# GpSimd's last shift of a D tile as one addition in place of a multiplication by 1.0 and an addition

## The chip, the core and the metric

The kernel runs on one core of a Trainium2 chip. The metric is the device time of one execution, in microseconds. The engines are TensorE (PE, matrix products; PEld is its loading of weights), VectorE (DVE), ScalarE (ACT), GpSimd (POOL) and SyncE (SP, which issues the transfers). They run their own lists of instructions in order and wait for one another through semaphores.

## What is computed

A residual block: x plus attention of the normalized x plus a dense layer with GELU of the same normalized x. There are 2048 rows of width 512, 32 query heads of width 16 over one shared key and value head, and a hidden width of 1792.

```python
x = A_x
xn = _layernorm(x, axis=-1)
return x + _A_ref(xn, A_wq, A_wk, A_wv, A_wo) + _B_ref(xn, B_w1, B_b1, B_w2, B_b2)
# _A_ref
scores = jnp.einsum("bhqd,bkd->bhqk", q, k) * (Dh ** -0.5)
p = _softmax(scores, axis=-1)
o = jnp.einsum("bhqk,bkd->bhqd", p, v)
# _B_ref
h = _gelu(jnp.einsum("bsd,df->bsf", h_in, w1) + b1)
return jnp.einsum("bsf,fd->bsd", h, w2) + b2
```

## The kernel before

**Tiles.** The scores are cut into tiles of 128 keys by 512 queries of one head. Four heads make a group; a group has 4 x 16 = 64 tiles, and 4 blocks of 512 queries by 8 groups make 32 groups, so there are 2048 tiles. They are worked off three at a time (`scores(u)`, `exp(u)`): three products into three banks of PSUM, with the two halves of six banks in turn.

**Two ways to the exponential.** `DTAB` says for each tile which engine turns its scores into weights. Most tiles go to ScalarE, which computes the exponential into `E` (L981). The others, the D tiles, go to VectorE: `p1` (L1012) turns the scores into 16-bit integers whose bits, read as bfloat16, are a rough power of two. One such number is too rough, so a D tile is used in five versions, each the first one plus a constant, and each multiplied by its own copy of V, already scaled by a constant of `SPL_C`. The sum of the five products makes a good exponential. The constants are `SPL_K = (-26, 0, 26, 51, 77)`.

**The shifts.** Up to six D tiles are collected in `batch`. `close_batch` then goes through three steps, each (out, in, number of buffers, constant):

```python
SPL_STEPS = ((1, 0, 1, 26), (2, 0, 2, 51), (0, 0, 1, -26))
```

The first two steps are VectorE's (L1059): buffer 1 becomes buffer 0 plus 26, and then buffers 2 and 3 become buffers 0 and 1 plus 51. The third step works in place: buffer 0 loses 26. It goes tile by tile (128 partitions by 512 int16), and by the program's rule it is GpSimd's (L1055, the kind `pl`). It can start once L1059 and TensorE have read the old buffer 0; after it, one more PV product per tile reads the new buffer 0.

**PV products.** `pv_mm` (L1025) adds V times a tile to the open bank `pO`, for four heads side by side. A product is planned by `allow=4.0`, as due 4.0 us after its operand is there. Buffer 0 is a ring of `ND = 19` tiles, the others are rings of `NR = 11`.

**What sets the order.** All work is first recorded by `add`, then `schedule` runs it through a table of planned durations and writes down each engine's list; `emit` turns the planned dependences into semaphore waits. For the shift the plan has `PL_OCC = 0.62` us. The planner places a GpSimd shift under a long VectorE instruction that reads PSUM (0.4 us or more), and has it wait until the VectorE instruction ahead (`gate`) has ended, so that GpSimd and VectorE's fast instructions between SBUF tiles (marked `lock`) do not overlap much. Where no such place is found in time, the planner gives the shift to VectorE: the same line, recorded with the same function. Of 557 shifts, 459 are on GpSimd and 98 on VectorE.

**Other work of GpSimd.** Two multiplications for each pair of groups (L1102), which divide the attention output by its sums, and the setting up of constants and masks in the first 28 us. Among the latter are the five scaled copies of V (L914, a multiplication by a constant), a mask times a number per partition (L921), a product with a constant for the layer norm (L762), all three with no second operation, and one small multiplication and addition (L722).

**The rest.** TensorE fits the projections of Q (L1139 empties them), the dense layer and the output projection in between, in the bank `pM`. A few products with zeros (L1336) stand where TensorE would pause.

Of the kernel before, what the change touches and what calls it, by code (L numbers as in the profile page):

```python
# [7 lines left out]
ALU = mybir.AluOpType  # L8
# [94 lines left out]
def vcost(n, mode=1):  # L103
    return n / 0.96e3 / mode + 0.065
# [7 lines left out]
class Prog:  # L112
# [19 lines left out]
    def add(self, eng, fn, r=(), w=(), acc=None, dma=None, occ=0.1, lat=0.15, allow=1.0, kind=None, tag=None, after=(), due=None, lock=False, docc=0.0):  # L132
        op = _Op()
        op.lock, op.docc = lock, docc
        op.eng, op.fn = eng, fn
        op.stream = dma or eng
        op.amt = 16 if dma else 1
        op.need = bool(dma)
        op.ticket = None
        op.occ, op.lat, op.allow, op.kind, op.tag = occ, lat, allow, kind, tag  # L140
        op.idx = len(self.ops)
        op.done = False
        op.due = due
        op.rel = None
        op.pm = any(k == ("bank", 7) or k[0] == ("bank", 7) for k in w)
        deps, sdeps = {}, {}

        def dep(o, raw):
            if o is None or o is op:
                return  # L150
            if o.stream == eng == "pe":
                sdeps.setdefault(id(o), (o, False))
                return
            deps[id(o)] = o
            sdeps[id(o)] = (o, True)

        for k in r:
            dep(self.writer.get(k), True)
            for o in self.accs.get(k, ()):
                dep(o, True)  # L160
        for k in w:
            dep(self.writer.get(k), False)
            for o in self.readers.get(k, ()):
                dep(o, False)
            for o in self.accs.get(k, ()):
                dep(o, False)
        if acc is not None:
            dep(self.writer.get(acc), False)
            for o in self.readers.get(acc, ()):
                dep(o, False)  # L170
        op.deps = list(deps.values())
        for o in op.deps:
            o.need = True
        for k in w:
            self.writer[k] = op
            self.readers[k] = []
            self.accs[k] = []
        for k in r:
            self.readers.setdefault(k, []).append(op)
        if acc is not None:  # L180
            self.accs.setdefault(acc, []).append(op)
        for o in after:
            sdeps.setdefault(id(o), (o, True))
        if self.in_chain:
            o = self.chain.get(eng)
            if o is not None:
                sdeps.setdefault(id(o), (o, False))
            self.chain[eng] = op
        op.sdeps = list(sdeps.values())
        self.ops.append(op)  # L190
        return op
# [344 lines left out]
def bass_parallel_sum__grouped_kv_mqa__dense_activation_gelu__prompt_kernel(  # L536
# [33 lines left out]
    with ExitStack() as es:  # L570
# [76 lines left out]
        add = pr.add  # L647
# [6 lines left out]
        def dve(fn, r=(), w=(), n=TBW, mode=1, allow=1.0, **kw):  # L654
            return add("dve", fn, r, w, occ=vcost(n, mode), lat=dlat[0], allow=allow, **kw)
# [27 lines left out]
        for i in range(8):  # L683
            e = X_Q[i]
# [251 lines left out]
        def tile_of(t):  # L936
            gg, r = divmod(t, TPG)
            return gg, r // HG, r % HG
# [26 lines left out]
        def exp(u):  # L965
# [20 lines left out]
            while ds:  # L986
                if not batch:
                    size[0] = bsize[ds[0][0]]
                n = 1
                while n < len(ds) and len(batch) + n < size[0] and ds[n][1] == ds[0][1] + n:  # L990
                    n += 1
                op = p1(ds[:n], ts[0] // TPG)
                o = o or op
                del ds[:n]
                if len(batch) == size[0] and batch[0][0] // TPG == ts[0] // TPG:
                    close_batch()
# [27 lines left out]
        def pv_mm(gg, j, v, kt, rhs, r):  # L1024
            add("pe", lambda e, a, b: e.matmul(pO[32 * j:32 * j + 32, :], V1[:, v, kt, :], rhs, start=a, stop=b,  # L1025
                                               tile_position=(0, 32 * j)),
                r=r + [("V", v, 0 if kt < NVA else NVA)], acc="O", occ=0.216, lat=dlat[1],
                allow=4.0 if gg < NTB * NGR - 1 or kt < NT - 4 else -5.0, kind="pv", tag=(gg, j))

        def close_batch():  # L1030
            n = len(batch)
            have = {0: 0}

            def slot(b):
                return base[0] if b == 0 else ND + (b - 1) * NR + base[1]

            def view(b, nb):
                s = slot(b)
                step = (slot(b + 1) - s if nb > 1 else n) * TBW
                return bass.AP(Dt[:].tensor, Dt[:].offset + s * TBW, [list(Dt[:].ap[0]), [step, nb], [1, n * TBW]])  # L1040

            def sums(bufs):
                for b in bufs:
                    v = 1 + SPL_K.index(have[b])
                    for q, (t, _) in enumerate(batch):
                        gg, kt, j = tile_of(t)
                        pv_mm(gg, j, v, kt, Dt[:, slot(b) + q, :].bitcast(bf), [(("D", base[b > 0] + q), b)])

            for o, i, nb, k in SPL_STEPS:
                def keys(b):  # L1050
                    return [(("D", base[b + m > 0] + q), b + m) for m in range(nb) for q in range(n)]
                if o == i:
                    for q in range(n):
                        d = Dt[:, slot(o) + q, :]
                        add("pool", lambda e, d=d, k=k: e.tensor_scalar(d, d, 1.0, float(k), ALU.mult, ALU.add),  # L1055
                            [], [(("D", base[o > 0] + q), o)], occ=PL_OCC, lat=PL_LAT, allow=PL_DUE, kind="pl", lock=True,
                            docc=vcost(TBW, 4))
                else:
                    dve(lambda e, d=view(o, nb), q=view(i, nb), k=k: e.tensor_scalar(d, q, float(k), None, ALU.add),  # L1059
                        r=keys(i), w=keys(o), n=nb * n * TBW, mode=4, allow=1.0, kind="post", lock=True)  # L1060
                for m in range(nb):
                    have[o + m] = have[i + m] + k
                sums(range(o, o + nb))
            del batch[:]
# [220 lines left out]
        for u in range(NU):  # L1285
            ts = list(range(3 * u, min(3 * u + 3, NTILE)))
            exp(u)
            if u + 2 < NU:
                scores(u + 2)
            for t in ts:  # L1290
                gg, kt, j = tile_of(t)
                if not is_d[t]:
                    pv_mm(gg, j, 0, kt, E[:, eslot[t], :], [("E", eslot[t])])
                if t % TPG == TPG - 1:
                    assert all(b[0] > t for b in batch)
                    if gg == NTB * NGR - 1:
                        o_norm_last(gg)
                    else:
                        o_evac(gg)
            for a in nextg:  # L1300
                pv_mm(*a)
            del nextg[:]
            if batch and len(batch) == size[0]:
                close_batch()
            for gu, tbs in GU:
                if u == gu:
                    gelu(tbs, u)
            n0 = len(pr.ops)
            while side and side[0][0] <= u:
                side.pop(0)[2]()  # L1310
            for op in pr.ops[n0:]:
                op.sdeps.append((exps[u], True))
                op.rel = exps[u]
# [61 lines left out]
```

## Time and profile before

| | us |
|---|---|
| median of 3 runs (747.54 to 747.80) | 747.73 |
| the profiled execution, its own time | 747.55 |
| its span, first to last instruction | 745.8 |
| granted TensorE clock over the span | 1.00 |
| PE, DVE, ACT busy | 731.8, 732.7, 730.9 |
| POOL busy | 391.4 |
| DMA, mean | 31 GB/s |

How to read the profile: a group's line names the code line, the engine, the operation, what is written and read with its shape, how many there are, the busy time in us and the mean of one in ns, and after the second bar the idle time of the engine just ahead of them and what ended it. A line of the waits names who waited for whom, the sum in us, how often, and the longest. A line of the timeline has the start and the length in us, the instruction, how many were merged into the row, and in brackets the idle time ahead. Spans on GpSimd are rough; the spacing of instructions that follow each other is safer than the length of one.

### The profile page before, as it was taken

How to read it: one execution, taken by the hardware profiler on the slowest of the kernel's cores; microseconds unless marked ns; L12 is line 12 of the kernel's file. 1: busy time of each engine (PE TensorE's matmuls, PEld its weight loads, DVE VectorE, ACT ScalarE, POOL GpSimd, SP SyncE). 2: the span in 40 equal slices, each digit the busy share in tenths (PEclk: the TensorE clock that was granted, in tenths of full speed). 3: DMA queues.
4: the chain of work that ended last, by engine and by line, in shares of the span. 5: the costliest groups of instructions: out<-in, count | busy, mean ns of one | idle time of the engine just before them, and what ended most of it. 6: DMA issues, size and time to landing. Idle time of an engine off the chain costs nothing.

```text
span 745.8 us, 22104 instructions
## 1 busy us (share of the span) xinstructions
PE 731.8 (98%) x9048; PEld 218.3 (29%) x9050; DVE 732.7 (98%) x1432; ACT 730.9 (98%) x743; POOL 391.4 (52%) x543
## 2 busy tenths in 40 slices
PE   7999999999999999999999999999999999999998
PEld 5322222222232222222232222322333222222223
DVE  8899999999999999999999999999999999999997
ACT  8899999999999999999999999999999999999995
POOL 5455555656433556555555455465564545646541
PEclk9999999999999999999999999999999999999999
DMA  9200100100010010100101010100100101010011
GB/s 312 66 9 24 32 8 18 24 10 16 16 46 22 18 39 17 25 16 16 27 10 28 25 38 17 37 18 12 23 16 19 34 18 38 16 40 23 11 31 36
DMA packets 32078, 23.34 MB, mean 31 GB/s; under 512 B 16369, under 2 KB 27498, under 8 KB 31978
## 3 DMA queue, kind: packets, MB, share of 16 engines
q1 hardware_dynamic: 30922, 21.90, 11.2%
q8 instruction: 72, 1.18, 0.7%
q14 instruction: 28, 0.23, 0.1%
q10 hardware_dynamic: 1056, 0.03, 0.1%
HBM read 13.08 MB, written 2.35 MB: 21 GB/s over the span
## 4 chain that ended last, share of the span: by engine, by line
ACT 61%; PE 30%; DVE 7%; issue 0%; DMA 0%; SPq 0%; POOL 0%
ACT E L981 60%; PE pAll L1025 13%; PE pAll L958 9%; PE pAll L672 7%; DVE Dt L1012 3%; DVE Dt L1059 2%; DMA x_sb<-in_A_x_dram 0%; DVE x_sb L1167 0%; ACT x_sb L1179 0%; PE pAll L810 0%; DVE stats L759 0%; ACT xnT L815 0%; PE pAll L666 0%; DVE Dt L1055 0%; DVE Of L1071 0%
## 5 line engine op out<-in xcount | busy, mean ns | idle before, releaser
L981 ACT ACTIVATE E<-pAll 128x1024 bf16<-128x1024 f32 (+1 forms) x677 | 680.0, 1263 | 1.9 <-PE pAll L958 1.8
L1055 POOL TENSOR_SCALAR Dt<-Dt 128x512 int16<-128x512 int16 x459 | 350.7, 764 | 303.1 <-DVE Dt L1059 128.4
L1025 PE MATMUL pAll<-Dt,V 128*32 128x512 bf16 x2785 | 406.2, 383 | 0.9 <-DVE Of L1071 0.5
L1012 DVE TENSOR_SCALAR Dt<-pAll 128x512 int16<-128x512 f32 (+1 forms) x545 | 368.6, 691 | 2.1 <-PE pAll L958 1.0
L1025 PE MATMUL pAll<-E,V 128*32 128x512 bf16 x1491 | 293.1, 383 | 0.0
L1059 DVE TENSOR_SCALAR Dt<-Dt 128x1024 int16<-128x1024 int16 (+5 forms) x560 | 292.3, 548 | 0.2
L958 PE MATMUL pAll<-QT,KT 32*128 32x512 bf16 x2048 | 267.1, 384 | 4.1 <-ACT E L981 0.9
L958 PEld LDWEIGHTS pAll<-QT,KT 32*128 32x128 bf16 x2048 | 66.7, 91 | 293.9 <-ACT E L981 283.1
L1025 PEld LDWEIGHTS pAll<-Dt,V 128*32 128x32 bf16 x2785 | 102.0, 95 | 101.5 <-issue 68.2
L672 PE MATMUL pAll<-xnT,w_sb 128*32 128x512 bf16 x896 | 85.0, 383 | 0.1
L1025 PEld LDWEIGHTS pAll<-E,V 128*32 128x32 bf16 x1491 | 69.4, 94 | 44.3 <-issue 32.2
L672 PE MATMUL pAll<-w_sb,x_sb 128*32 128x512 bf16 x448 | 68.0, 383 | 0.0
L672 PE MATMUL pAll<-w_sb,ub 128*32 128x512 bf16 x448 | 67.1, 383 | 0.2 <-DVE x_sb L1213 0.2
L672 PE MATMUL pAll<-wop,oTp 128*32 128x512 bf16 x256 | 56.8, 383 | 0.0
L1102 POOL TENSOR_TENSOR oTp<-OfP,rbP 128x256 bf16<-128x256 f32 x29 | 24.1, 837 | 27.2 <-DVE Dt L1055 14.6
L672 PEld LDWEIGHTS pAll<-xnT,w_sb 128*32 128x32 bf16 x896 | 22.1, 95 | 27.0 <-issue 16.3
L1055 DVE TENSOR_SCALAR Dt<-Dt 128x512 int16<-128x512 int16 x98 | 25.7, 281 | 0.0
L672 PE MATMUL pAll<-xnT,wq_sb 128*32 128x512 bf16 x256 | 23.2, 384 | 0.2 <-DVE ub L1167 0.2
L1071 DVE COPY Of<-pAll 128x512 f32<-128x512 f32 x31 | 21.1, 679 | 0.0
L1167 DVE TENSOR_SCALAR x_sb<-pAll,b1T 128x512 bf16<-128x512 f32 x28 | 20.7, 741 | 0.0
L1167 DVE TENSOR_SCALAR ub<-pAll,b1T 128x512 bf16<-128x512 f32 x28 | 20.7, 738 | 0.1
L672 PEld LDWEIGHTS pAll<-w_sb,x_sb 128*32 128x32 bf16 x448 | 16.8, 95 | 10.3 <-issue 7.9
(121 smaller groups left out, 261.9 us busy)
## 6 DMA issues: line engine op xcount, KB each, us to landing
OfP<-Of SPq DMA_DIRECT2D x124, 32.0 KB, 2.0
rbP<-rden_rows SPq DMA_DIRECT2D x124, 32.0 KB, 1.8
w_sb<-in_B_w_dram SPq DMA_DIRECT2D x2, 1792.0 KB, 12.8
x_sb<-in_A_x_dram SPq DMA_DIRECT2D x8, 256.0 KB, 4.3
x_sb<-in_A_x_dram SPq DMA_DIRECT2D x16, 128.0 KB, 2.2
QT<-qp SPq DMA_DIRECT2D x124, 16.0 KB, 1.8
out_dram<-x_sb SPq DMA_DIRECT2D x12, 128.0 KB, 1.9
wq_sb<-in_A_wq_dram SPq DMA_DIRECT2D x1, 512.0 KB, 6.2
```

Source lines behind the costliest of these rows:

```text
L672: add("pe", lambda e, c=c, j=j: e.matmul(o[c, :], l[:, c], rh, start=start, stop=stop, tile_position=(0, 32 * j)), r, [(k, j) for k in w] ...
L958: ins = e.matmul(o, l, rh, start=True, stop=True, tile_position=(q0, 0))
L981: o = act(lambda e: e.activation(E[:, s0:s0 + na, :], bank(b0, na).rearrange("p (a n) -> p a n", a=na), ACT.Exp, scale=LN2 / 128.0), w=[B( ...
L1012: op = dve(lambda e: e.tensor_scalar(Dt[:, s:s + n, :], bank(bk, n).rearrange("p (a n) -> p a n", a=n), float(127 * 128) + SPL_D, SPL_MIN, ...
L1025: add("pe", lambda e, a, b: e.matmul(pO[32 * j:32 * j + 32, :], V1[:, v, kt, :], rhs, start=a, stop=b, tile_position=(0, 32 * j)), r=r + [ ...
L1055: add("pool", lambda e, d=d, k=k: e.tensor_scalar(d, d, 1.0, float(k), ALU.mult, ALU.add), [], [(("D", base[o > 0] + q), o)], occ=PL_OCC, ...
L1059: dve(lambda e, d=view(o, nb), q=view(i, nb), k=k: e.tensor_scalar(d, q, float(k), None, ALU.add), r=keys(i), w=keys(o), n=nb * n * TBW, m ...
L1071: dve(lambda e: e.tensor_copy(Of[:, i, :], pO), w=["O", ("Of", i)], allow=0.0)
L1102: "pool", lambda e, c=c: e.tensor_tensor(oTp[0:n, sl, c], OfP[0:n, s, c], rbP[0:n, s, c], ALU.mult),
L1167: dve(lambda e: e.tensor_scalar(ubs[tb % 2][:, ft, :], pM, b1T[:, ft:ft + 1], None, ALU.add), r=["b1T"], w=M4 + [ukey(tb, ft)], n=TBW + 57 ...
```

## The change

One line of `close_batch`. The in-place shift was `d = d * 1.0 + k`, two operations in one instruction; it is now `d = d + k`, one operation with the second absent. `k` is -26.0, the tile is 128 x 512 int16, read and written in place. The planned durations stay as they are, and the instructions of all engines stand in the same order as before, 459 of the shifts on GpSimd and 98 on VectorE.

```diff
                 if o == i:
                     for q in range(n):
                         d = Dt[:, slot(o) + q, :]
-                        add("pool", lambda e, d=d, k=k: e.tensor_scalar(d, d, 1.0, float(k), ALU.mult, ALU.add),
+                        add("pool", lambda e, d=d, k=k: e.tensor_scalar(d, d, float(k), None, ALU.add),
                             [], [(("D", base[o > 0] + q), o)], occ=PL_OCC, lat=PL_LAT, allow=PL_DUE, kind="pl", lock=True,
                             docc=vcost(TBW, 4))
                 else:
```

## The prediction

> **What bounds the kernel now.** I read the page first (its span, its busy shares, its chain of waits), then the groups by line and shape, then the waits, then single instructions in the timeline.
>
> ```profile
> span 745.8 us, 22104 instructions
> PE 731.8 (98%) x9048; PEld 218.3 (29%) x9050; DVE 732.7 (98%) x1432; ACT 730.9 (98%) x743; POOL 391.4 (52%) x543
> ACT 61%; PE 30%; DVE 7%; issue 0%; DMA 0%; SPq 0%; POOL 0%
> ...
> L1055 POOL TENSOR_SCALAR Dt<-Dt 128x512 int16<-128x512 int16 x459 | 350.7, 764 | 303.1 <-DVE Dt L1059 128.4 <-PE pAll L1025 61.3 <-DVE Dt L1012 39.8
> L1055 POOL TENSOR_SCALAR Dt<-Dt x459: 620/622/2059, 28.0 to 732.8; 128x512 int16<-128x512 int16 x153
> ...
> PEld pAll L958 <- ACT E L981: 283.1, 658, 0.9
> PEld pAll L1025 <- POOL Dt L1055: 2.7, 12, 0.2
> ```
>
> Three engines are 98% busy at once: TensorE, VectorE and ScalarE feed one another in a closed ring (scores, exponential or D tile, PV product, next scores). GpSimd is busy 52% of the span, and it has no share of the chain. The changed instruction is the whole of that work in the steady part: 459 shifts, the first at 28.0 us. A shift alone takes 622 ns (the median); the mean is 764. GpSimd stood idle for 303.1 us ahead of them, mostly because the tile or VectorE was not ready. TensorE waited for a shift 12 times, 2.7 us in all. So today a shift is covered, with 303 us of room in the sum; what matters is its price after the edit.
>
> **The change.** It moves nothing: the same instructions stand in the same order on every engine, since the planner's figure for a shift stays 0.62 us. In each shift the pair of operations becomes one, an addition with no second operation. Ninety-eight of the shifts run on VectorE, written by the same line:
>
> ```profile
> L1055 DVE TENSOR_SCALAR Dt<-Dt 128x512 int16<-128x512 int16 x98 | 25.7, 281 | 0.0
> L1059 DVE TENSOR_SCALAR Dt<-Dt 128x512 int16<-128x512 int16 x120 | 32.5, 283 | 0.1
> ```
>
> L1059 is already the form with one addition, and at this shape it takes 283 ns against 281. I cost those 98 at nothing.
>
> On GpSimd no 128x512 int16 shift with one operation is in the trace, so I go by what GpSimd did with both forms at the start of the kernel. L722 has two operations; L762, L914 and L921 have one (a multiplication, second operation absent). The copies are there to see what the shape and the type cost.
>
> ```profile
> L722 POOL TENSOR_SCALAR isc<-mrow 128x1 f32<-128x1 f32 x1 | 0.2, 192 | 0.0
> L762 POOL TENSOR_SCALAR nm<-sm 128x1 f32<-128x1 f32 x3 | 0.7, 217 | 2.2 <-ACT oTp L756 2.1
> L713 POOL COPY oTp<-wvk 128x256 bf16<-128x256 bf16 x1 | 0.4, 407 | 0.0
> L717 POOL CAST ident_f<-ident 128x128 f32<-128x128 bf16 x1 | 0.3, 299 | 0.0
> L921 POOL TENSOR_SCALAR sel8R<-sel,R 128x128 bf16<-128x128 bf16 x1 | 0.6, 600 | 0.0
> ...
> 24.00 0.85 POOL L914 TENSOR_SCALAR V<-oTp 128x256 bf16<-128x256 f32 x1
> ```
>
> Take off the fixed part, which the rows of one element show, and divide by the rest of the elements. With two operations: (622 - 192)/511 = 0.84 ns for each element. Copy: (407 - 192)/255 = 0.84; cast: (299 - 192)/127 = 0.84. With one operation: L914, (850 - 217)/255 = 2.48 ns; L921, (600 - 217)/127 = 3.02 ns. One operation costs three times as much for each element as two. The shape is not the reason, since the copy of L713 writes runs of 16 as L914 does, and neither is a change of type, since the cast runs at 0.84. What L914 and L921 share, and the fast rows lack, is the absent second operation. They multiply while the new shift adds, and neither has int16, so the step could fail there.
>
> I take L914, whose scalar is a constant as in the shift (L921 reads its scalar from a tile): 217 + 511 x 2.48 = 1484 ns. The upper bound is L921's rate, 217 + 511 x 3.02 = 1760 ns. The lower bound is a shift that stays at 622 ns or falls to some 217 ns, if one operation on int16 saves all the work for each element.
>
> The GPSIMD Engine Reference of the Trainium skill, section 3.1 (side-by-side cycle accounting), speaks against this: a body of up to two operations runs at the port's 1.03 cycles per element. By that rule both forms cost the same and the time stays where it is. The trace agrees for the two-operation shift and differs for L914, at 2.48 ns; that reading is a rival below.
>
> Next, what surrounds a shift. Two in a row, the five of L914 against VectorE's fourfold-rate shifts, and one case of such a shift starting inside a GpSimd shift:
>
> ```profile
> 34.48 1.32 POOL L1055 TENSOR_SCALAR Dt<-Dt 128x512 int16<-128x512 int16 x2 [5.25 <-DVE Dt L1059]
> ...
> 24.93 0.85 POOL L914 TENSOR_SCALAR V<-oTp 128x256 bf16<-128x256 f32 x1
> 25.86 0.90 POOL L914 TENSOR_SCALAR V<-oTp 128x256 bf16<-128x256 f32 x1
> 25.12 0.35 DVE L1059 TENSOR_SCALAR Dt<-Dt 128x512 int16<-128x512 int16 x1
> 25.50 0.55 DVE L1059 TENSOR_SCALAR Dt<-Dt 128x1024 int16<-128x1024 int16 x1
> ...
> 162.92 0.62 POOL L1055 TENSOR_SCALAR Dt<-Dt 128x512 int16<-128x512 int16 x1
> 163.12 0.69 DVE L1059 TENSOR_SCALAR Dt<-Dt 128x1024 int16<-128x1024 int16 x1
> L1059 DVE TENSOR_SCALAR Dt<-Dt 128x1024 int16<-128x1024 int16 x201 | 82.9, 419 | 0.1
> ```
>
> Two shifts take 1.32 us, so 0.08 us lies between them. The mean of 764 ns against 622 is another 0.14 us of stretch, from VectorE's L1059 and L1055: at 162.92 the shift held VectorE off until it ended (0.69 us against 0.42). Inside the slow L914 at 24.93 it was milder. The first L1059 took 0.35 us against 0.28 and ended in the middle of L914; the second took 0.55 against 0.42; and the next L914 took 0.90 against 0.85. I take half of the stretch, 0.07 us, and a spacing of 1.484 + 0.08 + 0.07 = 1.63 us. VectorE's own delay, 0.07 and 0.13 us here for two operations, I count at nothing, because where shifts are dense VectorE waits for TensorE anyway; uncovered it would be 658 x 0.1 = 66 us.
>
> Over the whole run GpSimd must then serve 459 x 1.63 = 748 us of shifts in the 717.8 us left after 28.0. It becomes the slowest engine, and the 303 us of room is used up. The shifts also come in bunches. TensorE runs its list in order, and the planner puts a shifted tile's PV product at most 4 us after the shift (the `allow=4.0` of `pv_mm`). So lateness up to about that is absorbed; beyond it TensorE stands at that product, the next scores are late, and ScalarE and VectorE starve. I therefore count by stretches of 4 us, over 40 us from the middle (columns of the page by stretches: window, length, VectorE's busy time in L1055, GpSimd's in L1055):
>
> ```profile
> 300.00:304.00 4.00, 0.00 (x0) 1.21 (x2) 1.00 0.00 0
> 304.00:308.00 4.00, 0.28 (x1) 2.93 (x3) 1.00 0.11 25
> 308.00:312.00 4.00, 0.28 (x1) 2.45 (x5) 1.00 0.16 29
> 312.00:316.00 4.00, 0.79 (x3) 2.30 (x4) 1.00 0.27 62
> 316.00:320.00 4.00, 0.35 (x2) 1.19 (x2) 1.00 0.00 0
> 320.00:324.00 4.00, 0.00 (x0) 0.00 (x0) 1.00 0.09 18
> 324.00:328.00 4.00, 0.00 (x0) 1.62 (x2) 1.00 0.16 37
> 328.00:332.00 4.00, 0.28 (x1) 2.60 (x4) 1.00 0.07 17
> 332.00:336.00 4.00, 0.00 (x0) 2.98 (x4) 1.00 0.01 3
> 336.00:340.00 4.00, 0.00 (x0) 1.62 (x2) 1.00 0.02 4
> ```
>
> The sum is 18.90 us in 40, a little thinner than the run (350.7 in 717.8, 1.034 times as dense). Each busy time times 1.63/0.764 and times 1.034, that is 2.206, is what the stretch needs of GpSimd afterwards: 2.7, 6.5, 5.4, 5.1, 2.6, 0, 3.6, 5.7, 6.6, 3.6 us. Where it is under 4 us the stretch keeps its 4; the rest take what they need: 29.2 + 20 = 49.2 us for 40, a factor of 1.231. The sum is 28.0 + 717.8 x 1.231 = 912 us. The profiled execution was 747.55 us for a span of 745.8, so 1.75 us lies around it, and the median 747.73 is the same within 0.2 us. **Forecast: 913 us.** With L921's rate and the whole stretch (1.76 + 0.08 + 0.14 = 1.98 us) the same rows give a factor of 1.406 and 1039 us.
>
> **The rivals.**
>
> 1. *No change.* GpSimd does one int16 addition at the 0.84 ns of its copies, or the build makes the same instruction of both forms. For it: the fast rows include the only int16 ones, and the 303 us of room. Against it: every larger one-operation row. Time 747.7 us. It decides while the spacing stays under 0.764 x 4/(2.98 x 1.034) = 0.99 us, since then even the densest stretch fits.
> 2. *Faster.* The one-operation shift falls towards 217 ns. GpSimd isn't on the chain, so the gain is what TensorE waits for shifts, 2.7 us: 745 us. Nothing in the rows of one operation speaks for it.
> 3. *All lateness is absorbed.* The bunches are smoothed over much more than 4 us, since the D ring has 19 tiles. GpSimd then never idles: 28.0 + 459 x 1.56 + the 29 multiplications of L1102 = 28 + 717 + 27 + 1.75 = 774 us.
>
> ```profile
> L1102 POOL TENSOR_TENSOR oTp<-OfP,rbP 128x256 bf16<-128x256 f32 x29 | 24.1, 837 | 27.2 <-DVE Dt L1055 14.6 <-DVE Dt L1059 5.2 <-DVE Of L1071 3.1
> L1059 DVE TENSOR_SCALAR Dt<-Dt 128x1024 int16<-128x1024 int16 (+5 forms) x560 | 292.3, 548 | 0.2
> ```
>
> 4. *The longer shift shuts VectorE out for all of its length,* as at 162.92, so that GpSimd and VectorE's fast shifts take turns. Their sum adds 292.3 + 25.7 us to rival 3, less some 0.15 us of each of the 658 that lies under the other (0.42 of overlap cost 0.27): 774 + 318 - 99 = 993 us with GpSimd never idle, some 1100 with the idle time of the forecast; I take 1050. For it: 162.92. Against it: the L1059 that ended inside L914. The SBUF page of the Trainium skill (State Buffer, "Who interferes with whom") states it as a rule: the pair of ports goes to whoever starts first, for the whole instruction. The trace agrees at 162.92 and differs at 25.12.
> 5. *Every added nanosecond is exposed.* Shift, PV product, scores and the next shift form a loop with no room: 745.8 + 459 x (1.484 - 0.622) + 1.75 = 1143 us. Against it: TensorE waited for only 12 shifts so far.
>
> **How the numbers follow.** Forecast 0.55; rival 1: 0.09; rival 2: 0.04; rival 3: 0.11; rival 4: 0.15; rival 5: 0.06. A measurement of this kernel tells 0.2%, or 1.5 us, from no change, so faster is rival 2 (0.04), the same is rival 1 (0.09), and slower is the rest (0.87). The range goes from rival 3, rounded down, to rival 4's upper end: 770 to 1110 us. It leaves out rivals 1 and 2, most of rival 5 and a little of the edges, some 0.2.
>
> **What the new profile would show.** If the price is right, L1055 on GpSimd has a median near 1.5 us in place of 0.62, and the 98 on VectorE stay near 281 ns. If GpSimd is the new bound, its busy share is over 85%, the chain names L1055 on GpSimd, the row of TensorE's L1025 waiting for L1055 grows from 2.7 us to over 100, and ScalarE falls to about 80%. Rival 4 would show L1059 at 128x1024 well over 419 ns on the mean; by the forecast it stays under 0.6 us. What would make me wrong: a median of L1055 still near 0.62 us; L1055 long but TensorE's waits for it short (rival 3); or a granted clock below the 1.00 of every stretch above, because TensorE now pauses, which I have not priced.

## The result and the profile after

The changed kernel takes 1022.17 us (median of 4 runs, 1020.24 to 1025.96) against 747.75 us before. The ratio is 1.368, 95% interval 1.366 to 1.370: slower by 274 us. The profiled execution took 1025.96 us.

The page of the changed kernel, its span, busy shares, TensorE's granted clock in 40 slices, its chain and its first groups:

```profile
span 1024.2 us, 22104 instructions
PE 855.1 (83%) x9048; PEld 233.7 (23%) x9050; DVE 810.5 (79%) x1432; ACT 760.2 (74%) x743; POOL 835.8 (82%) x543
PEclk9988889888888898789889999988888999888999
POOL 38%; PE 27%; DVE 11%; issue 5%; SPq 0%; DMA 0%; ACT 0%; POOLq 0%
...
L1055 POOL TENSOR_SCALAR Dt<-Dt 128x512 int16<-128x512 int16 x459 | 796.5, 1735 | 145.9 <-PE pAll L1025 61.6
...
L1025 PE MATMUL pAll<-Dt,V 128*32 128x512 bf16 x2785 | 489.6, 415 | 153.1 <-POOL Dt L1055 149.7
L1059 DVE TENSOR_SCALAR Dt<-Dt 128x1024 int16<-128x1024 int16 (+5 forms) x560 | 345.3, 642 | 0.2
```

GpSimd stood outside the chain before; now its shift L1055 is the largest piece of it. No engine is busy more than 83%. The same 459 shifts take 796.5 us in place of 350.7. VectorE's L1059 grew by 53 us, and TensorE's clock is 0.898 on the mean.

The shift's own rows (least, median and most in ns) and VectorE's L1059 at one shape, then the waits of the changed kernel (sum in us, times, longest):

```profile
L1055 POOL TENSOR_SCALAR Dt<-Dt x459: 1487/1607/3292, 27.6 to 1011.3; 128x512 int16<-128x512 int16 x153
L1055 DVE TENSOR_SCALAR Dt<-Dt x98: 273/282/728, 86.3 to 1014.5; 128x512 int16<-128x512 int16 x98
...
L1059 DVE TENSOR_SCALAR Dt<-Dt 128x1024 int16<-128x1024 int16 x201 | 100.3, 506 | 0.1
```

```profile
ACT E L981 <- PE pAll L958: 235.2, 201, 4.7
PEld pAll L1025 <- POOL Dt L1055: 223.0, 181, 5.6
...
PE pAll L1025 <- POOL Dt L1055: 149.7, 139, 5.1
DVE Dt L1012 <- PE pAll L958: 135.7, 125, 5.7
```

TensorE stands at PV products whose shifted tile is late. It has two rows for this, one for the loading of weights (PEld, 223.0 us where it was 2.7) and one for the products (PE, 149.7 us). They lie over each other in time and must not be added. At 82.59, for instance, one shift ends both waits:

```profile
82.59 0.09 PEld L1025 LDWEIGHTS pAll<-Dt,V 128*32 128x32 bf16 x1 [2.92 <-POOL Dt L1055]
82.59 0.39 PE L1025 MATMUL pAll<-Dt,V 128*32 128x512 bf16 x1 [2.62 <-POOL Dt L1055]
```

The products stood idle for 1024.2 - 855.1 = 169.1 us in all, against 745.8 - 731.8 = 14.0 before, and 149.7 of that was for shifts. The next scores (L958) are then late, so ScalarE waits 235.2 us and VectorE 135.7 us for them. The span grew by 278 us; 155 of these are idle time of the products and 123 are busy time of the same 9048 products. These last longer (415 ns against 383 for those with D tiles), and fewer run side by side (4.4 on the mean in place of 4.7: the lengths of all products over the busy time). An undisturbed shift takes 1487 ns; the mean of 1735 is 248 ns more.

### The profile page after: what moved, and what is told of

It is laid out like the page before. It is cut to its first block, busy times and chain, and to the rows that moved or that the text cites. A ratio compares the mean times of both kernels' runs of the same rounds, so it can differ in the third digit from the quotient of the medians.

```text
span 1024.2 us, 22104 instructions
## 1 busy us (share of the span) xinstructions
PE 855.1 (83%) x9048; PEld 233.7 (23%) x9050; DVE 810.5 (79%) x1432; ACT 760.2 (74%) x743; POOL 835.8 (82%) x543
## 4 chain that ended last, share of the span: by engine, by line
POOL 38%; PE 27%; DVE 11%; issue 5%; SPq 0%; DMA 0%; ACT 0%; POOLq 0%
POOL Dt L1055 38%; PE pAll L1025 12%; PE pAll L958 8%; PE pAll L672 6%; DVE Dt L1012 5%; DVE Dt L1059 4%; DVE Dt L1055 1%; PE pAll L1336 1%; SPq L679 0%; DVE x_sb L1213 0%; DMA rden_rows<-den 0%; DVE Of L1071 0%; PE pAll L666 0%; DVE ub L1224 0%; DMA rbP<-rden_rows 0%
## 5 line engine op out<-in xcount | busy, mean ns | idle before, releaser
L1055 POOL TENSOR_SCALAR Dt<-Dt 128x512 int16<-128x512 int16 x459 | 796.5, 1735 | 145.9 <-PE pAll L1025 61.6
L981 ACT ACTIVATE E<-pAll 128x1024 bf16<-128x1024 f32 (+1 forms) x677 | 709.4, 1117 | 238.8 <-PE pAll L958 235.2
L1025 PE MATMUL pAll<-Dt,V 128*32 128x512 bf16 x2785 | 489.6, 415 | 153.1 <-POOL Dt L1055 149.7
L1012 DVE TENSOR_SCALAR Dt<-pAll 128x512 int16<-128x512 f32 (+1 forms) x545 | 371.2, 692 | 143.3 <-PE pAll L958 135.7
L1059 DVE TENSOR_SCALAR Dt<-Dt 128x1024 int16<-128x1024 int16 (+5 forms) x560 | 345.3, 642 | 0.2
L1025 PE MATMUL pAll<-E,V 128*32 128x512 bf16 x1491 | 321.4, 411 | 0.2 <-DVE Of L1071 0.2
L958 PE MATMUL pAll<-QT,KT 32*128 32x512 bf16 x2048 | 288.7, 417 | 6.5 <-DVE Dt L1012 4.2
L1025 PEld LDWEIGHTS pAll<-Dt,V 128*32 128x32 bf16 x2785 | 112.1, 97 | 332.6 <-POOL Dt L1055 223.0
L958 PEld LDWEIGHTS pAll<-QT,KT 32*128 32x128 bf16 x2048 | 68.3, 92 | 307.1 <-ACT E L981 170.3
L672 PE MATMUL pAll<-xnT,w_sb 128*32 128x512 bf16 x896 | 102.0, 449 | 0.0
L1071 DVE COPY Of<-pAll 128x512 f32<-128x512 f32 x31 | 21.3, 688 | 43.6 <-PE pAll L1025 39.6
L1055 DVE TENSOR_SCALAR Dt<-Dt 128x512 int16<-128x512 int16 x98 | 35.6, 382 | 0.0
L1179 ACT ACTIVATE x_sb<-x_sb 128x3584 bf16<-128x3584 bf16 x4 | 12.7, 3182 | 11.7 <-DVE x_sb L1167 11.7
```

The costliest lines, as they stand in the source:

```text
L672: add("pe", lambda e, c=c, j=j: e.matmul(o[c, :], l[:, c], rh, start=start, stop=stop, tile_position=(0, 32 * j)), r, [(k, j) for k in w] ...
L958: ins = e.matmul(o, l, rh, start=True, stop=True, tile_position=(q0, 0))
L981: o = act(lambda e: e.activation(E[:, s0:s0 + na, :], bank(b0, na).rearrange("p (a n) -> p a n", a=na), ACT.Exp, scale=LN2 / 128.0), w=[B( ...
L1012: op = dve(lambda e: e.tensor_scalar(Dt[:, s:s + n, :], bank(bk, n).rearrange("p (a n) -> p a n", a=n), float(127 * 128) + SPL_D, SPL_MIN, ...
L1055: add("pool", lambda e, d=d, k=k: e.tensor_scalar(d, d, float(k), None, ALU.add), [], [(("D", base[o > 0] + q), o)], occ=PL_OCC, lat=PL_LA ...
L1071: dve(lambda e: e.tensor_copy(Of[:, i, :], pO), w=["O", ("Of", i)], allow=0.0)
```

## The experiments

Unless it is said otherwise, each starts from the kernel before and changes what its diff shows. The diffs are cut down to the expression that changes, and `...` marks code or lines left out. The kernel before took 747.3 us beside all of them.

**1. Forms by themselves.** A kernel that runs only shifts. The lines of its profile are these, shortened:

```python
L63  pool.tensor_scalar(a, a, 1.0, -26.0, ALU.mult, ALU.add)
L66  pool.tensor_scalar(a, a, -26.0, None, ALU.add)      # L78, L81, L84: 128, 256, 1024 elements
L69  pool.tensor_scalar(a, a, -26.0, 0.0, ALU.add, ALU.add)
L72  pool.tensor_scalar(a, a, -26.0, 1.0, ALU.add, ALU.mult)
L75  pool.tensor_scalar(a, a, 1.0, None, ALU.mult)       # L90 bfloat16, L96 float32
L104 pool, L119 vector: eight of L66 beside 24 shifts of 128x1024 on VectorE
L108 pool, L124 vector: eight of L63 beside 24 shifts of 128x1024 on VectorE
L116 vector: eight such shifts alone
```

> Leaves out the whole computation: the output is a copy of x, and GpSimd and VectorE run shifts on scratch tiles. Theory (an absent second operation costs 2.48 ns for each element, present ones 0.84): 128x512 int16 with multiplication and addition 0.62 us, with one addition 1.48; addition and addition of 0 as well as addition and multiplication by 1 at 0.62; one multiplication 1.48; one addition on 128 elements 0.53, on 256 0.85, on 1024 2.76; bfloat16 and float32 the same as int16. Rival 1 (only the pair of multiplication and addition is fast): addition and addition 1.48 as well. Rival 2 (the type does it): int16 with one operation stays at 0.62 in this quiet place, and the length in the changed kernel comes from VectorE. Port: eight one-operation shifts beside VectorE's 128x1024 shifts (0.42 us alone). If the port is held for only a part of a shift, VectorE's mean is under 0.65 us; if for all of it, each shift lets at most one or two of them through and the mean is over 1 us.

Its groups on GpSimd:

```profile
L84 POOL TENSOR_SCALAR a<-a 128x1024 int16<-128x1024 int16 x4 | 11.1, 2767 | 0.3
L69 POOL TENSOR_SCALAR a<-a 128x512 int16<-128x512 int16 x4 | 7.7, 1924 | 0.3
L66 POOL TENSOR_SCALAR a<-a 128x512 int16<-128x512 int16 x4 | 6.0, 1491 | 0.3
L75 POOL TENSOR_SCALAR a<-a 128x512 int16<-128x512 int16 x4 | 5.9, 1492 | 0.1
L90 POOL TENSOR_SCALAR abf<-abf 128x512 bf16<-128x512 bf16 x4 | 5.9, 1488 | 0.1
L96 POOL TENSOR_SCALAR af<-af 128x512 f32<-128x512 f32 x4 | 5.8, 1488 | 0.1
...
L63 POOL TENSOR_SCALAR a<-a 128x512 int16<-128x512 int16 x4 | 2.5, 617 | 0.3
L72 POOL TENSOR_SCALAR a<-a 128x512 int16<-128x512 int16 x4 | 2.5, 617 | 0.3
...
L78 POOL TENSOR_SCALAR a<-a 128x128 int16<-128x128 int16 x4 | 2.1, 529 | 0.3
```

The rate of one operation is (2767 - 529)/896 = 2.50 ns for each element, and int16, bfloat16 and float32 are alike, so the expectation's rival 2, the type, is out. The order of multiplication and addition does not matter (617 both). But addition and addition is the slowest of all, 1924 ns. The theory had the price of the slow form right and its cause wrong: what the change lost is not a second operation but a pair that runs fast. The expectation's rival 1 had the side right and the price too low (1.48 us).

The same kernel's timeline, VectorE's shifts and GpSimd's in the two shared pieces and VectorE alone:

```profile
73.32 2.77 DVE L116 TENSOR_SCALAR c16b<-c 128x1024 int16<-128x1024 int16 x8 [68.20 <-POOL b L99]
76.01 8.13 DVE L119 TENSOR_SCALAR c16b<-c 128x1024 int16<-128x1024 int16 x24
76.59 8.89 POOL L104 TENSOR_SCALAR a<-a 128x512 int16<-128x512 int16 x1 [3.31 <-DVE c16b L116]
...
96.72 11.45 DVE L124 TENSOR_SCALAR c16b<-c 128x1024 int16<-128x1024 int16 x24
96.95 5.90 POOL L108 TENSOR_SCALAR b<-b 128x512 int16<-128x512 int16 x8 [0.62 <-DVE c16b L121]
```

Beside the slow form VectorE loses nothing: 8.13/24 = 0.34 us for each, as alone (2.77/8 = 0.35). GpSimd's first shift, which began while VectorE was at work, took 8.89 us: it ended at 85.48, only after VectorE's row had ended at 84.14. The other seven ran after that row, so only one slow shift was tried beside it. Beside the fast form the two engines took turns: GpSimd needed 5.90/8 = 0.74 us for each, and VectorE paid, 11.45 us in place of 8.13. The expectation had asked how long VectorE waits, and did not have GpSimd as the loser.

**2. Two additions in the kernel, and the other order.**

```diff
-e.tensor_scalar(d, d, 1.0, float(k), ALU.mult, ALU.add)
+e.tensor_scalar(d, d, float(k), 0.0, ALU.add, ALU.add)     # addition and addition
+e.tensor_scalar(d, d, float(k), 1.0, ALU.add, ALU.mult)    # the other order
```

> The shift as an addition of -26 and an addition of 0.0: two operations, without the multiplication. Theory (the absent second operation costs the time): a shift of 0.62 us on GpSimd and 747.7 us, within 1.5. Rival (only the pair of multiplication and addition has a fast path): 1.49 us for each shift and 1022 us.

> The shift as an addition of -26 and a multiplication by 1.0, the other order. Theory (the pair has the fast path in either order, and nothing but the length of the shift moves the kernel): 0.62 us for each shift and 747.3 us, within 1.5. Rival (something besides the length of a shift): a measurable difference.

Two additions took 1186.74 us, ratio 1.589 (1.586 to 1.591): slower than the change itself, as in experiment 1. The other order took 747.28 us, ratio 1.000 (0.999 to 1.001), with a median shift of 621 ns: the kernel before. The theory held for the second and fell for the first; the rival of the first had the side right and the price too low.

**3. More pairs by themselves.**

> Leaves out the whole computation: the output is a copy of x, and GpSimd alone runs shifts of 128x512 int16 with other operations. Theory after the first table (only a multiplication with an addition, in either order, has a fast path): 0.62 us for subtraction with multiplication and multiplication with subtraction at most; two multiplications, addition with subtraction, addition with minimum or maximum, maximum with minimum and multiplication with minimum all at 1.5 us or more; one subtraction and one maximum 1.49; one addition into another tile 1.49. Rival (two additions are a single bad pair, and other pairs are fast): most pairs 0.62 us.

Three groups of this kernel: L63 subtraction and multiplication, L69 two multiplications, L81 addition and maximum.

```profile
L63 POOL TENSOR_SCALAR a<-a 128x512 int16<-128x512 int16 x4 | 7.7, 1926 | 0.3
...
L69 POOL TENSOR_SCALAR a<-a 128x512 int16<-128x512 int16 x4 | 2.4, 618 | 0.1
...
L81 POOL TENSOR_SCALAR a<-a 128x512 int16<-128x512 int16 x4 | 7.7, 1919 | 0.3
```

Of the pairs tried, multiplication with addition in either order and two multiplications run at 617 to 618 ns. Every other pair takes 1.92 us: in this kernel also multiplication and subtraction, addition and subtraction, subtraction and addition, addition and minimum, maximum and minimum, multiplication and minimum (L66, L72, L75, L78, L84, L87, 1916 to 1924 ns). One operation takes 1.48 to 1.49: a subtraction (L90, 1491), a maximum (L93, 1484), an addition into another tile (L96, 1489). Subtraction in place of addition already loses the fast form. Two multiplications were expected among the slow ones: a miss.

**4. Half and three quarters of the shift.** Each leaves out the shift of the rest of the tile.

```diff
+e.tensor_scalar(d[:, 0:256], d[:, 0:256], float(k), None, ALU.add)   # half
+e.tensor_scalar(d[:, 0:384], d[:, 0:384], float(k), None, ALU.add)   # three quarters
```

> Leaves out the shift of the second half of each tile: one operation on 256 of the 512 elements, 217 + 255 x 2.48 = 0.85 us. Theory (lateness up to some 4 us is absorbed, GpSimd's own time decides from there): spacing 0.85 + 0.08 + 0.2 = 1.13 us, which by the stretches of 4 us gives 766 us, 750 to 790. Rival (every nanosecond of a shift over 0.62 us is exposed, 317 us for each us, from the two kernels): 820 us.

> Leaves out the shift of the last quarter of each tile: one operation on 384 elements, 217 + 383 x 2.48 = 1.17 us. Theory: spacing 1.17 + 0.08 + 0.25 = 1.50 us, by the stretches of 4 us 872 us, 840 to 900. Rival (every nanosecond exposed, 317 us for each us): 921 us.

The shift's group in the half, the three quarters and the two additions (a fence for each kernel):

```profile
L1055 POOL TENSOR_SCALAR Dt<-Dt 128x256 int16<-128x256 int16 x459 | 474.0, 1033 | 206.7 <-DVE Dt L1059 75.6 <-PE pAll L1025 53.8 <-DVE Dt L1012 14.6
```

```profile
L1055 POOL TENSOR_SCALAR Dt<-Dt 128x384 int16<-128x384 int16 x459 | 655.1, 1427 | 152.4 <-PE pAll L1025 55.3 <-DVE Dt L1059 36.5 <-PE pAll L672 9.1
```

```profile
L1055 POOL TENSOR_SCALAR Dt<-Dt 128x512 int16<-128x512 int16 x459 | 969.0, 2111 | 136.0 <-PE pAll L1025 67.7 <-DVE Dt L1059 20.6 <-PE pAll L958 4.6
```

| mean shift on GpSimd, ns | 764 (before) | 1033 (half) | 1427 (three quarters) | 1735 (the change) | 2111 (two additions) |
|---|---|---|---|---|---|
| kernel, us | 747.3 | 767.46 | 887.73 | 1022.17 | 1186.74 |
| us for each us of the mean, from the one before | | 75 | 305 | 436 | 438 |

If the growth of all 459 shifts were exposed, the last row would read 459. Up to 1.03 us five sixths of it is covered; from 1.4 us on, 95% of every further nanosecond is exposed. The theory's 766 and 872 us stand against 767.46 and 887.73; the rival's 820 and 921 are out. The edits shorten the 98 shifts on VectorE too, a small thing: they are busy 21.7 us at half length, 25.7 before and 35.6 in the change.

**5. The old form twice.** The shift by -26 as two by -13, one waiting for the other; on VectorE it stays single.

```diff
+e.tensor_scalar(d, d, 1.0, float(k) / 2, ALU.mult, ALU.add).then_inc(s_tw, 1)
+e.wait_ge(s_tw, n_tw[0])
+return e.tensor_scalar(d, d, 1.0, float(k) / 2, ALU.mult, ALU.add)
```

> Each GpSimd shift as two shifts by -13 of the old form, the second waiting for the first: 0.62 + 0.1 + 0.62 = 1.34 us, and the port held for nearly all of it. The 98 on VectorE stay single. Theory (the length of the shift decides, whatever its form): spacing 1.34 + 0.08 + 0.25 = 1.67 us, by the stretches of 4 us 926 us, 880 to 960. Rival (the form of the slow shift does something more to the other engines): well under 880, since the old form hides at any length. Rival (the port): over 1000 although the shift is shorter than 1.49 us, since VectorE is shut out for all of it.

It took 972.35 us, ratio 1.300 (1.299 to 1.302). Its two groups:

```profile
L1036 POOL TENSOR_SCALAR Dt<-Dt 128x512 int16<-128x512 int16 x459 | 353.7, 771 | 152.7 <-PE pAll L1025 59.4 <-DVE Dt L1070 36.0 <-PE pAll L672 8.7
L1039 POOL TENSOR_SCALAR Dt<-Dt 128x512 int16<-128x512 int16 x459 | 344.7, 751 | 38.0
```

A tile costs 0.771 + 0.083 (the 38.0 us of idle time over 459) + 0.751 = 1.605 us. A straight line between three quarters and the change gives 887.7 + (1.605 - 1.427) x 436 = 965 us for that. So the length of the work on GpSimd decides, and not its form, within these 7 us. The time lies 12 us above the theory's range (880 to 960) and under the 1000 of the rival with the port; the other rival, well under 880, is out too. The spacing was as expected (1.605 + 0.08 = 1.69 us against 1.67), so it is the count by stretches of 4 us that missed: it gives 931 us for the measured spacing.

**6. TensorE kept busy ahead of the waits.** The changed kernel, with eight products with zeros ahead of a PV product that waits for GpSimd.

```diff
...
+if len(seen) == 4 and any(s == "pool" for s, _ in op.waits):
+    for j in [0, 1, 2, 3] * NFILL:       # NFILL = 2
+        self.filler(eng, j, True)
...
 for s, t in op.waits:
     eng.wait_ge(sems[s], t)
```

> The change, with eight products with zeros (as those of L1336, 0.45 us) on TensorE ahead of each PV product that waits for a shift, where the bank is open in all four column groups. Theory of the clock (TensorE's pauses lower its granted clock to 0.90, and that costs some of the 109 us by which the forecast fell short): clock over 0.95 and 960 to 1005 us. Rival (the clock lies beside the wait for GpSimd and costs little): 1015 us or more, whatever the clock.

The granted clock rose from 0.898 to 0.981, and the time fell to 1002.43 us, ratio 1.341 (1.339 to 1.344), some 20 us below the change and inside the 960 to 1005 of the theory, near its upper end. A product of the scores (L958, here L968) took 384 ns before, 417 in the change and 389 here. The clock is a real part of the loss and a small one. The 20 us are a net sum: what the added products cost is in it, and the clock did not come back to 1.00.

**7. A plan that knows the length, and a plan without GpSimd.**

```diff
-PL_OCC = 0.62
+PL_OCC = 1.64          # with the changed shift
```

```diff
-add("pool", lambda e, d=d, k=k: e.tensor_scalar(d, d, 1.0, float(k), ALU.mult, ALU.add),
+dve(lambda e, d=d, k=k: e.tensor_scalar(d, d, float(k), None, ALU.add),
...
```

> The change, with the planner told 1.64 us for a shift in place of 0.62. The plan then has 248 shifts on GpSimd and 309 on VectorE, in a new order of all engines. Theory (the loss is TensorE standing at late shifts because the plan knows them as short): those waits nearly go, VectorE gains 211 x 0.28 = 59 us and becomes the bound again, 800 to 850 us. Rival (contention on the port with a one-operation shift, or the clock, is the loss): still over 900.

> All 557 shifts recorded as VectorE's, none on GpSimd; the plan makes a new order. VectorE's busy time is 732.7 + 459 x 0.281 = 862 us, and it is the bound: 850 to 885 us. So a one-operation shift on GpSimd (1022 us) costs more than having no help from GpSimd at all. Rival (the slow shift still helps VectorE): over 1022.

The first took 942.11 us, ratio 1.261 (1.259 to 1.263), 80 us better than the change, far from the 800 to 850 of the theory and on the side of its rival (over 900). It has 254 shifts on GpSimd and 303 on VectorE, where 248 and 309 were expected. Its waits:

```profile
ACT E L981 <- PE pAll L1025: 180.6, 30, 13.5
...
PEld pAll L1025 <- POOL Dt L1055: 19.2, 17, 4.9
PE pAll L1025 <- POOL Dt L1055: 12.5, 8, 4.6
```

The products' waits for shifts did go, from 149.7 to 12.5 us. VectorE's L1059 is at 296.0 us, near the 292.3 of the kernel before, and the clock at 0.988, so the rival has the number and not the reason: VectorE's delay and the clock are not the loss here. In place of the old waits came 30 long ones of ScalarE for PV products, 6 us each on the mean. All but two end within 2 us after the sums of a group are read out (L1071); why the new plan leaves them was not tried.

Without shifts on GpSimd the kernel took 857.96 us, ratio 1.148 (1.145 to 1.150), inside the expected 850 to 885. That is in part luck: VectorE is busy 826.4 us and not the 862 that were reckoned, and ScalarE waits here too for PV products, 33 times and 100.3 us in all. So a new order costs time of its own in both runs, and yet the slow shift on GpSimd is worse by 164 us than none there at all.

**8. The slow forms of the start.** The remaining one-operation rows of the kernel before, L914 and L921, each with an addition of 0.0 behind the multiplication.

```diff
-e.tensor_scalar(V1[:, 1 + v, :, 0:Dh], Vf, c, None, ALU.mult)
+e.tensor_scalar(V1[:, 1 + v, :, 0:Dh], Vf, c, 0.0, ALU.mult, ALU.add)
```

> The kernel before, with L914 and L921, two slow one-operation forms of the start, written with an addition of 0.0 behind the multiplication. Their rows fall from 865 to 0.41 us and from 600 to 0.3 us, some 2.6 us less of GpSimd ahead of 28 us. Theory (in the start TensorE and VectorE do not wait for GpSimd then): no change, 746.8 to 747.7 us. Rival (the copies of V hold up the first PV products): 1 to 2.5 us faster.

L914 fell from 865 to 407 ns and L921 from 600 to 376. The time was 747.39 us, ratio 1.000 (0.999 to 1.001): nothing that sets the time waits for GpSimd there, and the rival (1 to 2.5 us faster) is out. No run beat the kernel before.

## Why the prediction was right, and where it fell short

The forecast was 913 us in a range of 770 to 1110. The 1022 lie inside, but the loss is 274 us where 165 were forecast: the path was right, and the term of the sum that missed most is the stretch of a shift by VectorE.

- **The price of the shift.** Forecast 1484 ns, measured 1487 at the least. Right, and so rivals 1 and 2 are out. The reason given, an absent second operation, was wrong: two additions take 1924 ns. The number came out because L914, from which it was taken, is itself one operation. What the fast rows share is a pair with a fast path (experiments 1 to 3); the start of the kernel had no slow pair to show it.
- **The 98 shifts on VectorE.** Their median stayed at 282 ns, as said, but the mean went from 281 to 382, since some ran into a GpSimd shift.
- **GpSimd becomes the bound.** Right: it leads the chain, and the row of TensorE's weight loads waiting for it grew from 2.7 to 223.0 us, against "over 100" (149.7 in the row of the products). Its busy share is 82% where over 85% was said, and ScalarE fell to 74% rather than 80%; the span grew further than forecast. L1059 at 128x1024 took 506 ns on the mean, under the 0.6 us that was said.
- **The stretch, the term that was mis-sized.** The prediction took 0.07 us from the mild case at 24.93; it was 0.248. With a spacing of 1.487 + 0.08 + 0.248 = 1.815 us the prediction's own stretches of 4 us give 28.0 + 717.8 x 1.314 + 1.75 = 973 us: 60 of the missing 109 us. Half of the old stretch was taken because the slow L914 had been stretched little, but a longer shift meets more. A shift met 0.7 of VectorE's fast shifts (L1059 and L1055) on the mean before, and 1.5 in the changed kernel. The 111 slow shifts that met none took 1.49 us on the mean, the 125 that met one 1.69, and the 128 that met two 1.84.
- **The clock,** which the prediction named and left unpriced, is worth about 20 us (experiment 6).
- **The rest, some 29 us if the two parts add up, is not separated.** With the measured spacings the count by stretches of 4 us gives 764 us at half length, 874 at three quarters, 931 for the two shifts of experiment 5 and 973 for the change. It falls short of the runs by 3, 14, 41 and 49 us: the cover of 4 us is too generous for a longer shift, or VectorE's delay is missing. That delay, counted as nothing, was 53 us in L1059 and 10 in L1055, together close to the 66 us that the prediction gave for it uncovered. How much of it lies on the path, no run shows.
- **Rival 4,** the port held for the whole shift, was nearest in number (1050), but the shift shuts VectorE out for only a part of its length. The changed kernel's timeline shows a slow shift with a single L1059 starting inside it, early, in the middle and late:

```profile
1000.03 1.49 POOL L1055 TENSOR_SCALAR Dt<-Dt 128x512 int16<-128x512 int16 x1
1000.32 0.60 DVE L1059 TENSOR_SCALAR Dt<-Dt 128x1024 int16<-128x1024 int16 x1
...
564.84 1.49 POOL L1055 TENSOR_SCALAR Dt<-Dt 128x512 int16<-128x512 int16 x1
565.42 0.41 DVE L1059 TENSOR_SCALAR Dt<-Dt 128x1024 int16<-128x1024 int16 x1
...
281.11 1.49 POOL L1055 TENSOR_SCALAR Dt<-Dt 128x512 int16<-128x512 int16 x1 [2.76 <-PE pAll L1025]
282.15 0.99 DVE L1059 TENSOR_SCALAR Dt<-Dt 128x2048 int16<-128x2048 int16 x1
```

  At 0.29 us into the shift L1059 loses 0.18 us (0.60 against 0.42), at 0.58 nothing, and at 1.04 it loses 0.31 (0.99 against 0.68).
- **Rivals 3 and 5.** Lateness was not all absorbed, and not all exposed: 95% from 1.4 us on, a sixth up to 1.03 (experiment 4).

The GPSIMD Engine Reference of the Trainium skill, section 3.1, has a body of up to two operations bound by the port at 1.03 cycles per element. The runs agree for multiplication with addition (617 ns) and differ for two additions (1924) and one (1491). The SBUF page (State Buffer) of the Trainium skill, "Who interferes with whom", has the shared ports go to whoever starts first for the whole instruction. That fits the fast form, beside which VectorE's 24 shifts took 11.45 us in place of 8.13, and differs at 564.84, where L1059 ran inside a slow shift at its usual 0.41 us.

## What to carry to other kernels

Fewer operations in an instruction need not be cheaper: on GpSimd, price an instruction by a row with the same pair of operations, and time a few alternatives by themselves. An engine at 52% and off the chain can still become the bound: here the mean shift could grow from 0.76 to 1.03 us for 20 us of time, and past 1.4 us the kernel paid for 95% of each nanosecond. When an instruction gets longer, price also its meetings with another engine's instructions, because they grow with its length (0.7 to 1.5 for each shift here). The waits of two parts of one engine can lie over each other, so look at the timeline before you add them.

## What the runs showed of the hardware

- GpSimd's two-scalar instruction on 128x512: 617 to 618 ns for multiplication with addition in either order and for two multiplications, 1.92 us for every other pair tried, 1.48 to 1.49 us for one operation. Multiplication with addition and one multiplication were also timed in bfloat16 and float32, and took the same.
- A slow one-operation shift of 1.49 us keeps VectorE's fast shifts out in two stretches and lets them run in between. Of the slow shifts of the changed kernel that met a single one of them: the 9 that began 0.21 to 0.45 us into it lost 0.03 to 0.26 us against the median of their shape; the 16 at 0.47 to 0.89 lost under 0.01; the 25 at 0.95 to 1.33 lost 0.03 to 0.40. Why it does so, no run shows.
- Beside an unbroken row of VectorE's shifts it mattered which form GpSimd ran: eight shifts of the fast form made VectorE wait (8.13 to 11.45 us for 24), while the one slow shift that began inside the row waited for all of it (8.89 us).
